# A new hand-set order for one attention and mixture-of-experts kernel, with one small product moved to a bank of its own

## The chip, the cores and the metric

The kernel runs on one core of a Trainium2 chip. The metric is the device time of one execution in microseconds (us), median of three runs.

## The reference

Attention with a sliding window of 96 keys and 8 global keys, biased by distance, over 4 batches of 8 heads with 768 positions of 64 elements; then a soft mixture of 8 experts with 4 slots each on its output.

```python
scores = scale * np.matmul(q, k.transpose(0, 1, 3, 2))
keep = is_global | is_local
bias = -slopes[:, None, None] * dist[None, :, :]
scores = np.where(keep, scores + bias, -1000000000.0)
a = np.exp(scores - np.max(scores, axis=-1, keepdims=True))
a = a / (np.sum(a, axis=-1, keepdims=True) + 1e-09)
x = np.matmul(a, v)                      # to (3072, 512), heads side by side
logits = x @ phi                         # 32 slots
d = softmax of logits over the rows      # dispatch
slot_input = d.T @ x
slot_out[e] = np.maximum(slot_input[e] @ w1[e], 0.0) @ w2[e]
out = (softmax of logits over the slots) @ slot_out
```

The window's sizes come as an integer input n (`n_global`, `n_local`), read on the device.

## The kernel before

**Two stages.** The first is attention, in 16 units u of two heads each (i = 0, 1); four units make a batch. The second, the tail, has the experts' two layers and the combination; its code is the same in both kernels and is no part of ORDER.

**Steps of one unit.** Each step is a small function that issues a few instructions:

- `load_qk`, `load_v`: one DMA each on SP's queue, into two buffers in turn (units 2 and 3 borrow weight buffers).
- `scores(u, k)`, k = 0 to 2: TensorE, 4, 4 and 6 products (two rows each in the trace, as they are float32) into one of two PSUM tiles `sc` (L535).
- `biased(u, k)`: VectorE adds a bias table to `sc`, keeps the running maximum, and writes `tb` in SBUF (L544, custom operation). One operand is in PSUM, one in SBUF.
- `max_t` (TensorE, L551) and `max_r` (VectorE, L556) turn the maximum into a bias, `exponential(u, i)` and `w_hi(u, i)` (ScalarE, L560 and L563) make exp and its float16 rounding `ph`.
- `w_lo(u, i, part)`, three parts: the rest, exp minus its rounding, 128x432 elements, two operands that both lie in SBUF (L570). `w_lo` is GpSimd's, `w_lo_dve` the same instruction on VectorE.
- `v_hi` (GpSimd, L503) or `v_hi_act` (ScalarE, L506): float16 rounding of the values; `v_lo` (VectorE, L513): the rest, again two operands in SBUF, 128x896.
- `values(u, i)`: TensorE, 39 products into bank i of the PSUM tile `x` (L587). `x` is one tile of two banks, used by all units.
- `ev_sums`, `ev_recs`: row sums and reciprocals (L600, L606). `ev_mul(u, i)`: VectorE scales bank i of `x` into `xn` and frees it (L612). These are the two scalings of a unit.
- `tr`, `tr_copy` (ScalarE, L629) or `tr_copy_dve` (VectorE, L633): transposition of `xn`; `logits` (L654).
- Each fourth unit: `logits_all` (L671), `strip_max` (L688), `strip_exp`, `strip_sum` (L705), `by_token`, `dispatch`, `dispatch_sum`: the running softmax over rows.

**At the start** `bcast` converts n and spreads it over 128 partitions with a 1-row product; `keys` reads that product and makes the limits (L816 to L818, L257 to L259), `table_even` and `table_odd` make the first bias table (L264, L268) that `biased(0, 0)` reads. `warm` issues products of ones of 512 columns, which nobody reads, into `x`; `WARM` such products stand ahead of everything (L439). In the kernel before, `bcast` writes to bank 1 of `x`, and `keys` reads it there.

**Weights.** `piece` loads a weight piece of 1 MB into a buffer of its own, `extra` loads a part of one into a corner that attention never uses (0.12 to 0.26 MB), `free` loads one into an attention buffer that is needed no more. All go by SP's one queue, in the order in which they are issued.

**What sets the order.** `ORDER` is a list of 608 steps, written out by a planner and fixed in the file. Every engine has its instructions in the order of this list, and waits by semaphores for what the others write or read. A reader or writer of a tile waits for the last step ahead of it in the list that used that tile in a conflicting way; `x` counts as one tile in this, so an `ev_mul(u, 1)` that stands behind `values(u + 1, 0)` in the list waits for that product, though it reads the other bank.

Of the kernel before, what the change touches and what calls it, by code (L numbers as in the profile page):

```python
# [49 lines left out]
WARM = 12  # L50
# [233 lines left out]
def tile_attention_moe(ctx: ExitStack, tc: tile.TileContext, qk, v, phi, w1, w2, nn, out):  # L284
    nc = tc.nc
# [70 lines left out]
    held = []  # L356
    for name, i, *_ in ORDER:
        if name == "free":
# [71 lines left out]
    ones = keep.tile([P, P], F32, name="ones")  # L430
# [6 lines left out]
    busy_in = nc.const_aps.tensor(1.0, [P, 512], BF16)  # L437
    for _ in range(WARM):
        nc.tensor.matmul(out=wp[0:1], lhsT=busy_in[:, 0:1], rhs=busy_in, start=True, stop=True)  # L439

    table = BiasTable(nc, tabs, xn01)
    nf = keep.tile([1, 4], F32, name="nf")
# [10 lines left out]
    def late_constants():  # L453
        nc.gpsimd.tensor_tensor(out=i4, in0=ident[:, 0:32], in1=ident[:, 32:64], op=ALU.add)
        nc.gpsimd.tensor_tensor(out=i4, in0=i4, in1=ident[:, 64:96], op=ALU.add)
        nc.gpsimd.tensor_tensor(out=i4, in0=i4, in1=ident[:, 96:128], op=ALU.add)
        nc.gpsimd.memset(sl, 0.0)
# [15 lines left out]
    xx = psx.tile([P, 2, 512], F32, name="x", tag="x")  # L473
    mxs, nbs, rcs, ms = {}, {}, {}, {}
# [6 lines left out]
    def bank(key):  # L481
        if key in LAST_BANKS:
            k, i = LAST_BANKS[key]
            return sc[k][:, i]
        return psm.tile([P, 512], F32, name="m", tag="m")

    class LeftBanks:

        n = 0
# [320 lines left out]
    def bcast(u):  # L810
        nc.vector.tensor_copy(out=nf, in_=nraw)
        nc.tensor.matmul(out=xx[:, 1, 0:4], lhsT=ones[0:1], rhs=nf, start=True, stop=True)

    def keys(u):
        words = xx[:, 1, 0:4].rearrange("p (i w) -> p w i", w=2)
        nc.vector.tensor_scalar(out=nlt, in0=words[:, 0], scalar1=0.0, scalar2=None, op0=ALU.is_lt)  # L816
        nc.vector.tensor_tensor(out=nlt, in0=nlt, in1=words[:, 1], op=ALU.add)
        nc.vector.scalar_tensor_tensor(out=nv, in0=nlt, scalar=2.0 ** 32, in1=words[:, 0], op0=ALU.mult, op1=ALU.add)  # L818
        table.keys(ngl, nlo)
# [10 lines left out]
    def table_pair(p):  # L830
        table.pair(p)

    steps = dict(piece=piece_of, free=free, extra=extra, load_qk0=load_qk0, load_phis=load_phis, bcast=bcast, keys=keys, table_rest=table_rest, warm_x=warm_x, warm=warm,
                 table_even=table_even, table_odd=table_odd, table_pair=table_pair, load_qk=load_qk, load_v=load_v, v_hi=v_hi, v_hi_act=v_hi_act, v_hi_dve=v_hi_dve, v_lo=v_lo,
                 scores=scores, biased=biased, max_t=max_t, max_r=max_r, exponential=exponential, w_hi=w_hi, w_lo=w_lo, w_lo_dve=w_lo_dve, w_hi_dve=w_hi_dve,
                 values=values, ev_sum=ev_sum, ev_rec=ev_rec, ev_sums=ev_sums, ev_recs=ev_recs, ev_mul=ev_mul, tr=tr, tr_copy=tr_copy, tr_copy_dve=tr_copy_dve,
                 logits=logits, logits2=logits2, logits_half=logits_half, logits_all=logits_all, strip_max=strip_max, strip_exp=strip_exp,
                 strip_sum=strip_sum, by_token=by_token, by_token_copy=by_token_copy, lnat_copy=lnat_copy, dispatch=dispatch, dispatch_sum=dispatch_sum)
    late_constants()
    for name, u, *args in ORDER:  # L840
        steps[name](u, *args)
# [291 lines left out]
```

## Time and profile before

| | |
|---|---|
| median of three runs | 209.16 us (208.80 to 209.75) |
| the profiled execution, its own time | 210.29 us |
| its span, first to last instruction | 208.4 us |
| mean granted TensorE clock | 0.958 |
| busy: TensorE, VectorE, ScalarE, GpSimd | 84%, 74%, 59%, 52% |
| attention, about | 0 to 146.6 us |
| tail, about | 146.6 to 208.4 us |

The shares are means over the whole span; attention and tail differ, and the rows below are cut by stretch. A row's "idle before" names what ended an engine's wait. Waits of an engine for a shared resource do not show as idle time in these rows: the instruction is counted as busy from its start, and becomes longer.

### The profile page before, as it was taken

How to read it: one execution, taken by the hardware profiler on the slowest of the kernel's cores; microseconds unless marked ns; L12 is line 12 of the kernel's file. 1: busy time of each engine (PE TensorE's matmuls, PEld its weight loads, DVE VectorE, ACT ScalarE, POOL GpSimd, SP SyncE). 2: the span in 40 equal slices, each digit the busy share in tenths (PEclk: the TensorE clock that was granted, in tenths of full speed). 3: DMA queues.
4: the chain of work that ended last, by engine and by line, in shares of the span. 5: the costliest groups of instructions: out<-in, count | busy, mean ns of one | idle time of the engine just before them, and what ended most of it. 6: DMA issues, size and time to landing. Idle time of an engine off the chain costs nothing.

```text
span 208.4 us, 6316 instructions
## 1 busy us (share of the span) xinstructions
PE 176.1 (84%) x2612; PEld 127.7 (61%) x2612; DVE 154.9 (74%) x382; ACT 122.1 (59%) x157; POOL 107.9 (52%) x127
## 2 busy tenths in 40 slices
PE   8879998988898999899597998698799999998400
PEld 2346777867687788788466886566443345865400
DVE  4386999998999898989798989994577804653700
ACT  3007788995958879989594889861404521531500
POOL 6302978997994988899684988790000000000000
PEclk9975999999999999999999999999999999999955
DMA  6984087499996699975948998899969999677892
GB/s 204 401 309 170 12 272 297 156 333 421 374 350 250 228 349 397 349 242 175 338 163 273 406 371 287 293 333 346 351 281 306 407 414 425 267 255 255 293 335 95
DMA packets 18761, 61.39 MB, mean 295 GB/s; under 512 B 1570, under 2 KB 8994, under 8 KB 16546
## 3 DMA queue, kind: packets, MB, share of 16 engines
q1 hardware_dynamic: 18720, 60.89, 80.1%
q8 instruction: 22, 0.36, 0.7%
q14 instruction: 17, 0.14, 0.2%
q10 hardware_dynamic: 2, 0.00, 0.0%
HBM read 54.59 MB, written 6.29 MB: 292 GB/s over the span
## 4 chain that ended last, share of the span: by engine, by line
PE 54%; DVE 28%; issue 5%; POOL 4%; DMA 3%; ACT 1%; DVEq 0%; POOLq 0%
PE x L587 11%; PE sc L535 11%; PE x L139 7%; DVE tb L544 7%; PE hp L106 7%; DVE v L513 5%; DVE xn L612 4%; POOL ph L570 3%; DMA raw<-in_qk_dram 3%; DVE ph L570 3%; PE m L624 3%; PE wp L439 3%; PE cp L199 2%; PE ctp L173 2%; PE x L524 2%
## 5 line engine op out<-in xcount | busy, mean ns | idle before, releaser
L570 POOL TENSOR_TENSOR ph<-tb,ph 128x432 f16<-128x432 f32 x82 | 92.6, 1160 | 29.3 <-ACT ph L563 28.9
L560 ACT ACTIVATE tb<-tb,nb 128x1296 f32<-128x1296 f32 x32 | 43.6, 1374 | 17.1 <-DVE nb L556 17.0
L587 PE MATMUL x<-v,ph 128*128 128x65 f16 (+1 forms) x1248 | 43.2, 193 | 6.7 <-DVE xmax L612 5.8
L587 PEld LDWEIGHTS <-ph 128*128 128x128 f16 x1248 | 41.0, 97 | 11.3 <-issue 6.0
L563 ACT CAST ph<-tb 128x1296 f16<-128x1296 f32 x32 | 40.5, 1270 | 12.6 <-PE x L587 11.3
L535 PE MATMUL sc<-raw 64*128 64x216 f32 (+1 forms) x392 | 42.7, 354 | 3.9 <-DVE mx L544 2.9
L535 PEld LDWEIGHTS sc<-raw 64*128 64x128 f32 x392 | 33.5, 195 | 11.5 <-DVE mx L544 4.9
L612 DVE CUSTOM_DVE_ANT_1 xn<-x,rc 120x448 f32<-120x448 f32 x32 | 19.4, 622 | 3.8 <-PE x L587 3.3
L513 DVE SCALAR_TENSOR_TENSOR v<-vt,v 128x896 f16<-128x896 f32 x14 | 19.3, 1377 | 0.8 <-POOL v L503 0.8
L544 DVE CUSTOM_DVE_ANT_1 tb<-sc,tt,mx 128x864 f32<-128x864 f32 x16 | 17.8, 1110 | 2.0 <-PE sc L535 1.1
L624 PE MATMUL m<-ident,xn 120*128 120x120 f32 x105 | 15.7, 275 | 1.9 <-DVE xmax L612 1.4
L570 DVE TENSOR_TENSOR ph<-tb,ph 128x432 f16<-128x432 f32 x14 | 14.4, 1032 | 0.0
L624 PEld LDWEIGHTS m<-ident,xn 120*128 120x128 f32 x105 | 10.8, 141 | 4.8 <-issue 2.1
L139 PE MATMUL x<-wp,wp 128*32 128x256 f32 x96 | 10.7, 380 | 0.0
L106 PE MATMUL hp<-wp,sl 128*32 128x512 f32 x80 | 10.5, 593 | 0.0
L503 POOL TENSOR_SCALAR v<-vt 128x896 f16<-128x896 f32 x9 | 9.6, 1065 | 1.0 <-PE x L587 1.0
L544 DVE CUSTOM_DVE_ANT_1 tb<-sc,xtt,mx 128x864 f32<-128x864 f32 x8 | 8.9, 1111 | 0.3
L544 DVE CUSTOM_DVE_ANT_1 tb<-sc,xta,mx 128x864 f32<-128x864 f32 x8 | 8.9, 1110 | 0.1
L544 DVE CUSTOM_DVE_ANT_1 tb<-sc,tt 128x864 f32<-128x864 f32 x8 | 8.4, 1052 | 0.0
L139 PE MATMUL x<-ph,wp 128*32 128x256 f32 x32 | 7.3, 380 | 0.0
L139 PE MATMUL x<-tb,wp 128*32 128x256 f32 x32 | 7.2, 379 | 0.0
L199 PE MATMUL cp<-sots,ct 128*128 128x256 f32 x48 | 6.6, 291 | 0.6 <-DVE sots L185 0.6
(207 smaller groups left out, 280.6 us busy)
## 6 DMA issues: line engine op xcount, KB each, us to landing
wp<-in_w_dram SPq DMA_DIRECT2D x11, 1024.0 KB, 9.0
raw<-in_qk_dram SPq DMA_DIRECT2D x13, 832.0 KB, 6.9
vt<-in_v_dram SPq DMA_DIRECT2D x14, 448.0 KB, 5.8
wp<-in_w_dram SPq DMA_DIRECT2D x10, 512.0 KB, 6.6
tb<-in_w_dram SPq DMA_DIRECT2D x4, 1024.0 KB, 7.5
raw<-in_w_dram SPq DMA_DIRECT2D x2, 1024.0 KB, 13.9
out_dram<-tb SPq DMA_DIRECT2D x4, 512.0 KB, 3.5
out_dram<-xtt SPq DMA_DIRECT2D x4, 512.0 KB, 7.0
```

The costliest lines, as they stand in the source:

```text
L106: nc.tensor.matmul(out=hp[n][32 * s:32 * s + 32, :], lhsT=slv(a, c, s), rhs=w1(e, c // 2)[:, (c % 2) * DF + 512 * n:(c % 2) * DF + 512 * n ...
L139: nc.tensor.matmul(out=o[32 * s:32 * s + 32, 0:w], lhsT=ht[:, c, 32 * s:32 * s + 32], rhs=w2(4 * a + s, half)[:, c0 + c * w:c0 + c * w + w ...
L199: nc.tensor.matmul(out=cp[:, w * k:w * k + w], lhsT=ct[:, t * P:t * P + P], rhs=sot, start=True, stop=True)
L513: nc.vector.scalar_tensor_tensor(out=vlo[k].rearrange("p j i d -> p (j i) d"), in0=vraws(u).rearrange("p j i d -> p (j i) d"), scalar=V_SC ...
L535: nc.tensor.matmul(out=z[:, i, at:at + n], lhsT=r_[r, KCOL[j]:KCOL[j] + KR], rhs=r_[r, KW + KB * j:KW + KB * j + n], start=True, stop=True)
L544: nc.vector.tensor_tensor_reduce(out=tb(u)[:, :, BW * k:BW * k + BW], in0=sc[(3 * u + k) % 2][:, :, 0:BW], in1=table.unit(u % NP, k), scal ...
L560: nc.scalar.activation(out=t, in_=t, func=AF.Exp, bias=nbs[u], scale=T_SC)
L563: nc.scalar.copy(out=blocks(phi_[i])[:, :, 0:QW], in_=tb(u)[:, i].rearrange("p (s c) -> p s c", c=QW))
L570: (engine or nc.gpsimd).tensor_tensor(out=blocks(plo_[i])[:, c, 0:QW], in0=tb(u)[:, i].rearrange("p (s c) -> p s c", c=QW)[:, c], in1=bloc ...
L587: nc.tensor.matmul(out=x[:, (D + 1) * t:(D + 1) * t + d], lhsT=w[:, c:c + P], rhs=vv[:, j, i, 0:d], start=(z == 0), stop=(z == len(ops) - ...
L612: nc.vector.tensor_tensor_reduce(out=xnb[(u // 2) % 3][:, :, c:c + D], in0=xv[:, i, :, 0:D], in1=rcs.pop((u, i)).unsqueeze(2).to_broadcast ...
L624: nc.tensor.transpose(out=m[:, at:at + KB], in_=xnb[(u // 2) % 3][:, t, P * (p % 2):P * (p % 2) + P], identity=ident[0:KB, 0:KB])
```

## The change

`ORDER` holds the same steps in another order, and some go to another engine. Counted in the two lists:

| step | before | after |
|---|---|---|
| `w_lo` on GpSimd / `w_lo_dve` on VectorE | 82 / 14 | 78 / 18 |
| `v_hi` on GpSimd / `v_hi_act` on ScalarE | 10 / 6 | 8 / 8 |
| `tr_copy` on ScalarE / `tr_copy_dve` on VectorE | 29 / 3 | 27 / 5 |
| products of `warm` in ORDER / of WARM | 14 / 12 | 17 / 6 |
| units whose `ev_mul` stands behind the next unit's first `values` | 7 | 0 |
| `extra` steps ahead of the first load of q and k | 0 | 2 |

```diff
-WARM = 12
-ORDER = [('load_qk0', 0), ('bcast', 0), ('warm', 0, 2), ('scores', 0, 0), ('load_qk', 0), ('warm', 0, 1),
...
+WARM = 6
+ORDER = [('bcast', 0), ('keys', 0), ('extra', 4), ('extra', 5), ('load_qk0', 0), ('warm', 0, 2), ('scores', 0, 0),
...
     def bcast(u):
         nc.vector.tensor_copy(out=nf, in_=nraw)
-        nc.tensor.matmul(out=xx[:, 1, 0:4], lhsT=ones[0:1], rhs=nf, start=True, stop=True)
+        ms["n"] = m = bank(("n", u))
+        nc.tensor.matmul(out=m[:, 0:4], lhsT=ones[0:1], rhs=nf, start=True, stop=True)
 
     def keys(u):
-        words = xx[:, 1, 0:4].rearrange("p (i w) -> p w i", w=2)
+        words = ms.pop("n")[:, 0:4].rearrange("p (i w) -> p w i", w=2)
```

`bank` gives one of the two PSUM banks `m` that transpositions and logits use.

**VectorE at the start, `bcast` and `keys`**, as a difference (x is the tile of the values and of the warm products, m a bank of its own):

```order
 L811 CAST nf<-nraw 1x4 [waits DMAHW0_49]
-L816 TENSOR_SCALAR nlt<-x 128x2 [waits PE_49]
-L817 TENSOR_TENSOR nlt<-nlt,x 128x2 [waits DVE_49]
-L818 SCALAR_TENSOR_TENSOR nv<-nlt,x 128x2 [waits DVE_49]
+L817 TENSOR_SCALAR nlt<-m 128x2 [waits PE_49]
+L818 TENSOR_TENSOR nlt<-nlt,m 128x2 [waits DVE_49]
+L819 SCALAR_TENSOR_TENSOR nv<-nlt,m 128x2 [waits DVE_49]
```

The rows are the same but for the tile: the first waits now for the product that wrote m alone, and no more for warm products that write x.

**SP's queue at the start**, before (raw, wp of in_qk are q and k, vt are values):

```order
L400 DMA raw_93<-in_qk_dram 128x592
L404 DMA raw_93<-in_qk_dram 128x432
L404 DMA raw_93<-in_qk_dram 128x640
L404 DMA raw_94<-in_qk_dram 128x1664
L404 DMA wp_91<-in_qk_dram 128x1664
L407 DMA vt<-in_v_dram 128x896
L404 DMA wp_92<-in_qk_dram 128x1664
L407 DMA vt<-in_v_dram 128x896 [waits DMAHW0_49]
```

and now:

```order
L387 DMA raw_93<-in_w_dram 128x384
L387 DMA raw_94<-in_w_dram 128x384
L400 DMA raw_93<-in_qk_dram 128x592
L387 DMA vt<-in_w_dram 128x256
L404 DMA raw_93<-in_qk_dram 128x432
L404 DMA raw_93<-in_qk_dram 128x640
L387 DMA xn_105<-in_w_dram 128x256
L404 DMA raw_94<-in_qk_dram 128x1664 [waits DMAHW0_49]
L407 DMA vt<-in_v_dram 128x896 [waits DMAHW1_49]
L387 DMA ph_98<-in_w_dram 128x512 [waits DMAHW2_49]
L404 DMA wp_92<-in_qk_dram 128x1664 [waits DMAHW3_49]
L387 DMA wp_83<-in_w_dram 128x2048 [waits DMAHW4_49]
```

Parts of weights (in_w) moved in front of and between the loads of q and k.

**VectorE around the scalings of unit 6**, before (L612 into xn is a scaling, L513 is `v_lo`):

```order
L600 TENSOR_TENSOR rsall<-x,eps 120x14 [waits PE_49]
L606 RECIPROCAL rc<-rsall 120x14 [waits DVE_49]
L556 ISA m,nb<-m,shift 128x128 [waits PE_49]
L556 ISA nb 128x1
L612 ISA xn_106,xmax<-x,rc 120x7x64 [waits DVE_49]
L612 ISA xmax 120x1
L513 SCALAR_TENSOR_TENSOR v_100<-vt,v_100 128x896 [waits DMAHW4_49]
L544 ISA tb_97,mx<-sc_177,xtt,mx 128x2x432 [waits PE_49]
L544 ISA mx 128x1
L612 ISA xn_106,xmax<-x,rc 120x7x64 [waits PE_49]
L612 ISA xmax 120x1
```

and now:

```order
L544 ISA tb_95,mx<-sc_171,tt,mx 128x2x432 [waits DVE_49,PE_49]
L544 ISA mx 128x1
L750 COPY sacc<-m 128x512 [waits PE_49]
L612 ISA xn_106,xmax<-x,rc 120x7x64
L612 ISA xmax 120x1
L612 ISA xn_106,xmax<-x,rc 120x7x64
L612 ISA xmax 120x1
L544 ISA tb_96,mx<-sc_170,xta 128x2x432 [waits PE_49,Activation_49,Pool_49]
L544 ISA mx 128x1
L513 SCALAR_TENSOR_TENSOR v_100<-vt,v_100 128x896 [waits DMAHW1_49,Activation_49]
```

The second scaling moved up to the first and lost its wait for TensorE.

## Rows read from the trace of the kernel before

**Rows 1.** Stretches: length, busy PE PEld DVE ACT POOL (count), clock, DMA share, GB/s.

```profile
0.00:13.00 13.00, 10.12 (x48) 4.48 (x49) 6.50 (x25) 1.76 (x3) 5.13 (x35) 1.00 0.87 325
13.00:19.00 6.00, 6.00 (x24) 2.93 (x26) 4.65 (x11) 2.24 (x2) 0.00 (x0) 0.54 0.64 235
...
22.00:140.00 118.00, 104.47 (x1879) 87.25 (x1878) 110.30 (x260) 96.35 (x112) 100.00 (x90) 1.00 0.81 292
...
146.60:208.40 61.80, 46.71 (x540) 26.60 (x536) 28.63 (x76) 17.00 (x34) 0.00 (x0) 0.91 0.83 307
```

**Rows 2.** Groups by line and shape, columns: count | busy us, mean ns | idle before.

```profile
L570 POOL TENSOR_TENSOR ph<-tb,ph 128x432 f16<-128x432 f32 x82 | 92.6, 1160 | 29.3 <-ACT ph L563 28.9 <-DVE mx L544 0.3
L503 POOL TENSOR_SCALAR v<-vt 128x896 f16<-128x896 f32 x9 | 9.6, 1065 | 1.0 <-PE x L587 1.0
...
L513 DVE SCALAR_TENSOR_TENSOR v<-vt,v 128x896 f16<-128x896 f32 x14 | 19.3, 1377 | 0.8 <-POOL v L503 0.8
L570 DVE TENSOR_TENSOR ph<-tb,ph 128x432 f16<-128x432 f32 x14 | 14.4, 1032 | 0.0
L513 DVE SCALAR_TENSOR_TENSOR v<-wp,v 128x896 f16<-128x896 f32 x2 | 2.9, 1426 | 0.0
```

**Rows 3.** Single lines, columns: count, duration in ns as minimum/median/maximum, first and last start.

```profile
L513 DVE SCALAR_TENSOR_TENSOR v<-vt,v x14: 1086/1192/1921, 23.1 to 134.6; 128x896 f16<-128x896 f32 x14
L570 DVE TENSOR_TENSOR ph<-tb,ph x14: 603/1098/1456, 39.3 to 139.4; 128x432 f16<-128x432 f32 x14
L570 POOL TENSOR_TENSOR ph<-tb,ph x82: 997/1009/1940, 19.5 to 139.3; 128x432 f16<-128x432 f32 x82
L705 DVE SCALAR_TENSOR_TENSOR state<-state,al x3: 214/908/967, 105.9 to 149.4; 128x1 f32<-128x1 f32 x3
L544 DVE CUSTOM_DVE_ANT_1 tb<-sc,xtt,mx x8: 1104/1110/1119, 29.7 to 128.0; 128x864 f32<-128x864 f32 x8
L633 DVE COPY xtt<-m x1: 651/651/651, 86.9 to 86.9; 128x480 f32<-128x480 f32 x1
```

**Rows 4.** Instructions in order of time, 134 to 140 us, columns: start, us, engine.

```profile
134.57 5.72 POOL L570 TENSOR_TENSOR ph<-tb,ph 128x432 f16<-128x432 f32 x5 [1.37 <-ACT ph L563]
134.61 1.92 DVE L513 SCALAR_TENSOR_TENSOR v<-vt,v 128x896 f16<-128x896 f32 x1
```

**Rows 5.** Waits: who waited for whom, columns: total us, times, longest us.

```profile
DVE xn L612 <- PE x L587: 3.3, 4, 1.4
PE x L587 <- DVE xmax L612: 5.8, 9, 1.9
```

**Rows 6.** Instructions in order of time, 99 to 102 us, the false wait.

```profile
99.87 1.33 PE L587 MATMUL x<-v,ph 128*128 128x65 f16 x39 [0.22 <-DVE xmax L612]
101.24 0.62 DVE L612 CUSTOM_DVE_ANT_1 xn<-x,rc 120x448 f32<-120x448 f32 x1 [1.43 <-PE x L587]
```

**Rows 7.** Instructions in order of time, 0 to 17 us.

```profile
0.77 5.28 PE L439 MATMUL wp<-const-bfloat16-1.0 128*1 128x512 bf16 x12 [0.77 <-PEq L1120]
3.10 0.34 DVE L811 CAST nf<-nraw 1x4 f32<-1x4 int32 x1
5.98 0.58 PE L812 MATMUL x<-nf,ones 1*128 1x4 f32 x2
7.05 1.00 PE L535 MATMUL sc<-raw 64*128 64x216 f32 x8
8.40 0.16 DVE L816 TENSOR_SCALAR nlt<-x 128x2 f32<-128x2 f32 x1 [4.96 <-PE x L524]
10.80 1.06 DVE L544 CUSTOM_DVE_ANT_1 tb<-sc,tt 128x864 f32<-128x864 f32 x1
13.45 1.81 PE L535 MATMUL sc<-raw 64*128 64x216 f32 x8
```

**Rows 8.** Issue of the first DMA of q and k: count, KB, us to landing.

```profile
raw<-in_qk_dram SPq DMA_DIRECT2D x1, 296.0 KB, 2.9
```

**Rows 9.** The chain that ended last, 36 to 48 us, columns: start, us, what.

```profile
38.14 6.54 DMA raw<-in_qk_dram
```

2 lines of the change are left out of this document (1 added, 1 removed).

## The prediction

> **What bounds the kernel now.** I read the stretches first, then the groups by line, then single durations, the waits, and the start in order of time. The stretches [rows 1] show two regimes. From 146.6 us on the tail takes 61.8 us; its code is not touched, so it counts as fixed and the change must pay in attention. From 22 to 140 us VectorE is busy 110.3 of 118 us, TensorE 104.5, GpSimd 100.0, ScalarE 96.4: VectorE is the fullest engine, and nobody has much room. From 13 to 19 us the granted clock is 0.54, so that eight score rows that took 1.00 us at 7.05 take 1.81 us at 13.45 [rows 1, 7].
>
> VectorE's busy time is not all work. `v_lo` takes 1.09 us at best and 1.92 us at worst, `w_lo` 0.60 and 1.46 us on VectorE, 1.00 and 1.94 us on GpSimd [rows 3]. `biased` stays within 1.10 to 1.12 us [rows 3], though GpSimd works beside it most of the time. What tells them apart is that `v_lo` and `w_lo` have two operands in SBUF, `biased` one. The order of time shows how: a `v_lo` that starts 0.04 us behind a GpSimd subtraction takes 1.92 us, about one GpSimd instruction (1.01) plus its own 1.09 less the overlap of start and end [rows 3, 4]. So the two engines take turns, instruction by instruction, and whoever comes second waits inside its own busy time. Summed, with the shortest duration as the work: `v_lo` 22.2 us busy - 16 x 1.09 = 4.8 us of waiting; VectorE's `w_lo` 14.4 - 14 x 0.603 = 6.0; two of the three state sums (L705) 0.91 and 0.97 for 0.21 = 1.4. VectorE waits 12.2 us in 32 instructions, 0.38 each; GpSimd's `w_lo` wait 92.6 - 82 x 1.009 = 9.9 us [rows 2, 3].
>
> Put end to end, this exclusive work is 82 x 1.009 + 10 x 1.065 on GpSimd and 17.4 + 8.4 on VectorE, 119 us, in the about 121 us from 19.5 to 140.3 [rows 2, 3]. Starts and ends overlap a little, so the turn-taking is not full, but it is the fullest resource of all.
>
> **Start.** The 12 products of WARM start 0.44 us apart (5.28 / 12) and `bcast`'s product follows at 5.98 [rows 7]. Six fewer free it 2.6 us sooner; the converted n is there at 3.44 [rows 7], so the product can start near 3.5 and end at 4.1. Then `keys` waits for nothing else: the 4.96 us wait on warm products in x goes [rows 7]. From `keys` to the first `biased` took 10.80 - 8.40 = 2.4 us, so the table is there at 6.5. The other input is `scores(0, 0)`. Its 296 KB landed 2.9 us after their issue [rows 8]; now two parts of weights of 192 KB (384 columns of float32) go first: two issues of about 0.45 us and 0.39 MB, which at 325 GB/s [rows 1] is 1.2 us if it all adds. I take landing at 5.0 (4.5 to 5.7), the scores 1.0 to 1.8 us later, and the first `biased` at 6.8 in place of 10.80: 4 us ahead. Not all of it reaches the steady part, since the next scores wait for more of q and k behind two more weight parts, and since the clock may be half from the beginning: three score blocks at 1.81 for 1.00 are 2.4 us. If the clock instead never falls from 13 to 19 us, up to 5 blocks x 0.8 = 4 us come on top, less what the load order takes. Ends -0.7 and -6; I take **-3.5 us**, near the undisturbed 4.
>
> **Work moved.** Four `w_lo` more on VectorE: +4 x 0.603 = 2.4 us there, -4 x 1.009 = 4.0 on GpSimd. Two `tr_copy_dve` more: at most +2 x 0.65 = 1.3 us [rows 3]. Two `v_hi` move from GpSimd (-2 x 1.065 = 2.1) to ScalarE, which has 21 us free [rows 1, 2]. VectorE gets +3.7 us of work, and the exclusive work falls by 4.0 + 2.1 - 2.4 = 3.7 us.
>
> **Scalings ahead of the next product.** In seven units the second `ev_mul` stood behind the next unit's first product and waited for it. At 101.24 VectorE waits 1.43 us for a product that started at 99.87 [rows 6]; four such waits sum to 3.3 us [rows 5]. They go. The price: in those seven units the next `values` now starts after the second scaling as well, 0.54 us later where TensorE was waiting already; it does wait there, 5.8 us in 9 times [rows 5]. That is 0 to 7 x 0.54 = 3.8 us on TensorE, which has 13.5 us of room in the stretch; I take **+1.0 us** on the end.
>
> **Two-operand work apart.** The trace of before can't show how well the new order separates it. One bound: nothing gained, 36 instructions at 0.38 (the two state sums aside) = 13.7 us of waiting, +1.5 more than now. The other: all 12.2 us gone. I take half, 6 us: the order of both engines is fixed and they hang together through ScalarE and TensorE, but a turn is 1 us long, and half a turn of drift undoes a placement. So VectorE's time in the stretch changes by +3.7 - 3.3 - 6 = -5.6 us. It does not all reach the end, because the chain there alternates between TensorE and VectorE; half is 2.8. The exclusive work, the other candidate for the bound, falls by 3.7. Both point to **-3.0 us** (ends +1.9 and -8).
>
> [...]
>
> **End of attention and tail.** Of unit 15's six `w_lo` GpSimd does three in place of five, VectorE three in place of one: 5 x 1.009 + 0.603 = 5.6 us in turn becomes 4.8. As the last products wait for them I take **-0.5 us**. Weights come earlier in SP's queue (`extra` and `piece` steps moved forward), and the tail's own loads are unchanged: 0.
>
> **Sum.** -3.5 + 1.0 - 3.0 - 0.5 = -6.0 us against the profiled execution's 210.29, so 204.3. That execution is 1.13 us above the median of the three runs, 209.16; on that scale the forecast is **203.2 us**, for its own case 201.5 to 205.
>
> **Rivals.** *The separation is perfect*: all 12.2 us go, VectorE's stretch falls by 3.7 - 3.3 - 12.2 = -11.8, half reaches the end, -5.9 in place of -3.0: 200.3. For it: the durations fall into two clear levels [rows 3], so a planner can know them. Against: drift. *The clock stays half from the start*, since the warm-up is halved: the lead is 4 - 2.4 = 1.6 us in place of 3.5: 205.1. For it: the clock was low after a pause of TensorE already [rows 1, 7]; against: ORDER has three more warm products among the first scores. [...] *The loads become the wait*: weight pieces go between the loads of q and k, and one such load already holds the chain for 6.54 us [rows 9]. If half the start's lead (1.8) and half the steady gain (1.5) are spent waiting for q and k, 206.5. Against: DMA is busy 0.81 of the steady stretch [rows 1], and all ten pieces come early, so the later loads have a freer queue. *Slower: the order comes apart at run time.* Turns are granted as before, 0.38 us a piece: VectorE +3.7 - 3.3 + 1.5 = +1.9, all of it passed on as the engine is full; the seven later products cost their 3.8; the lead shrinks to 1.6; the end gives 0.5: +3.6, so 212.8. It decides once drift exceeds about half a turn, 0.5 us, at most placements. That the change does nothing is no case: the start's wait is gone for certain.
>
> **How the numbers follow.** Forecast 0.42, perfect separation 0.15, low clock 0.15, loads 0.18, order comes apart 0.10. About 0.5% (1.05 us) is what a measurement can tell from no change. Faster by more holds the first three wholly and most of the fourth: 0.82; within 0.5%, its rest and a mild form of the last, 0.09; slower 0.09. The range, 199.2 to 208.2, takes in the first four with their unknown terms and leaves out the best of the second and the slower case.
>
> **What would show it.** First `biased` near 6.8 us, not 10.8; granted clock from 13 to 19 us above 0.54; `v_lo` on average below 1.25 us and VectorE's `w_lo` below 0.85 (now 1.38 and 1.03); no wait of L612 for L587; VectorE's busy time up to the end of attention a few us lower, and attention's end near 140.5; the tail unchanged at 61.8 us. The forecast is wrong if `v_lo` and `w_lo` keep their means, if TensorE's waits for q and k or for the scalings grow past 5 us, or if the tail starts to wait for weights.

## The result and the profile after

The changed kernel takes 202.84 us (median of four runs, 201.58 to 204.56), the kernel before 209.45 us beside it (208.80 to 210.02): a ratio of 0.969, 95% interval 0.961 to 0.977. The forecast was 203.2 us. Ratios, here and below, leave out runs over 1.5% longer than the fastest of the same kernel, which matters for one version alone (e9, four of its six runs). The profiled execution of after took 204.56 us, with a span of 202.6 in place of 208.4; the readings below compare these two spans, which differ by 5.8 us.

The stretches of after, to be held against [rows 1] (length, busy PE PEld DVE ACT POOL with counts, clock, DMA share, GB/s):

```profile
0.00:13.00 13.00, 9.05 (x44) 4.48 (x44) 7.62 (x27) 1.95 (x4) 5.33 (x35) 0.90 0.83 278
13.00:19.00 6.00, 6.00 (x45) 3.63 (x43) 4.88 (x12) 4.00 (x4) 0.52 (x1) 0.93 1.01 417
...
140.60:202.60 62.00, 46.97 (x542) 26.69 (x540) 28.54 (x76) 16.80 (x33) 0.00 (x0) 0.91 0.85 316
```

The clock from 13 to 19 us is 0.93 where it was 0.54, the DMA share there 1.01 where it was 0.64. From 10 to 13 us it went the other way, 0.58 in place of 1.00, and the third block of scores took 1.95 us in place of 1.08. Attention ends at 140.6 in place of 146.6, and the tail takes 62.0 us, as before (61.8). The start of after, in order of time (start, us, engine), answers [rows 7]:

```profile
3.58 0.38 PE L813 MATMUL m<-nf,ones 1*128 1x4 f32 x2
4.01 0.16 DVE L817 TENSOR_SCALAR nlt<-m 128x2 f32<-128x2 f32 x1 [0.57 <-PE m L813]
...
6.77 1.06 DVE L544 CUSTOM_DVE_ANT_1 tb<-sc,tt 128x864 f32<-128x864 f32 x1
...
9.32 1.00 PE L535 MATMUL sc<-raw 64*128 64x216 f32 x8 [1.96 <-DMA raw<-in_qk_dram]
...
10.36 1.12 DVE L544 CUSTOM_DVE_ANT_1 tb<-sc,tt,mx 128x864 f32<-128x864 f32 x1 [2.08 <-PE sc L535]
...
10.56 1.95 PE L535 MATMUL sc<-raw 64*128 64x216 f32 x12
```

The first `biased` starts at 6.77 us, 4.0 us ahead. Then the second block of scores waits 1.96 us for its part of q and k, VectorE waits 2.08 us for that block, and the fourth `biased` starts at 15.55, only 1.0 us ahead of the 16.55 of before.

From that fourth `biased` to the end of attention, before and after (columns as above):

```profile
16.55:146.60 130.05, 115.70 (x2017) 94.77 (x2015) 117.59 (x277) 103.31 (x121) 102.81 (x92) 0.99 0.79 287
```

```profile
15.55:140.60 125.05, 113.70 (x2018) 94.20 (x2015) 119.01 (x283) 103.66 (x120) 95.66 (x86) 1.00 0.80 297
```

So of the 5.8 us the start kept 1.0, the stretch gave 5.0, and the tail took 0.2 back. In the stretch VectorE is busy no less than before (119.01 against 117.59). What fell is its time without work: 130.05 - 117.59 = 12.5 us, now 125.05 - 119.01 = 6.0. GpSimd is busy 7.2 us less.

The groups of two-operand work (count | busy us, mean ns | idle before) and their single lines (minimum/median/maximum in ns), to be held against [rows 2, 3]:

```profile
L570 POOL TENSOR_TENSOR ph<-tb,ph 128x432 f16<-128x432 f32 x78 | 86.8, 1145 | 30.4 <-ACT ph L563 30.0
...
L513 DVE SCALAR_TENSOR_TENSOR v<-vt,v 128x896 f16<-128x896 f32 x14 | 19.4, 1383 | 0.0
...
L570 DVE TENSOR_TENSOR ph<-tb,ph 128x432 f16<-128x432 f32 x18 | 16.2, 916 | 0.0
```

```profile
L513 DVE SCALAR_TENSOR_TENSOR v<-vt,v x14: 1078/1090/1894, 20.8 to 131.1; 128x896 f16<-128x896 f32 x14
L513 DVE SCALAR_TENSOR_TENSOR v<-wp,v x2: 1565/1668/1772, 31.3 to 37.1; 128x896 f16<-128x896 f32 x2
```

Counted as the prediction did, with 1.09 us and 0.603 us as the work: `v_lo` waits 14 x 1.383 + 2 x 1.668 - 17.4 = 5.3 us inside itself, VectorE's `w_lo` 18 x 0.916 - 18 x 0.603 = 5.6. That is 10.9 us in 34 steps, where it was 4.8 + 6.0 = 10.8 us in 30: 0.32 us a step after 0.36. The waiting in turns is what it was. Waits of TensorE (total us, times, longest us), beside [rows 5]; no row of L612 waiting for L587 is left:

```profile
PE sc L535 <- DMA raw<-in_qk_dram: 3.9, 3, 2.0
...
PE x L587 <- DVE xmax L612: 2.2, 5, 0.6
```

### The profile page after: what moved, and what is told of

Same layout as the page of the kernel before. It is cut to its first block, busy times and chain, and to the rows that moved or that the text cites. A ratio compares the mean times of both kernels' runs of the same rounds, so it can differ in the third digit from the quotient of the medians.

```text
span 202.6 us, 6321 instructions
## 1 busy us (share of the span) xinstructions
PE 172.3 (85%) x2609; PEld 126.9 (63%) x2609; DVE 156.6 (77%) x388; ACT 123.2 (61%) x157; POOL 101.0 (50%) x121
## 4 chain that ended last, share of the span: by engine, by line
## 5 line engine op out<-in xcount | busy, mean ns | idle before, releaser
L570 POOL TENSOR_TENSOR ph<-tb,ph 128x432 f16<-128x432 f32 x78 | 86.8, 1145 | 30.4 <-ACT ph L563 30.0
L587 PE MATMUL x<-v,ph 128*128 128x65 f16 (+1 forms) x1248 | 43.4, 193 | 5.9 <-POOL ph L570 2.4
L587 PEld LDWEIGHTS <-ph 128*128 128x128 f16 x1248 | 41.2, 97 | 8.8 <-issue 3.8
L535 PE MATMUL sc<-raw 64*128 64x216 f32 (+1 forms) x392 | 41.1, 346 | 4.0 <-DMA raw<-in_qk_dram 3.9
L535 PEld LDWEIGHTS sc<-raw 64*128 64x128 f32 x392 | 33.0, 192 | 11.6 <-issue 5.7
L513 DVE SCALAR_TENSOR_TENSOR v<-vt,v 128x896 f16<-128x896 f32 x14 | 19.4, 1383 | 0.0
L612 DVE CUSTOM_DVE_ANT_1 xn<-x,rc 120x448 f32<-120x448 f32 x32 | 18.9, 620 | 0.5
L570 DVE TENSOR_TENSOR ph<-tb,ph 128x432 f16<-128x432 f32 x18 | 16.2, 916 | 0.0
L506 ACT ACTIVATE v<-vt 128x896 f16<-128x896 f32 x7 | 6.6, 948 | 11.1 <-DMA vt<-in_v_dram 11.1
L503 POOL TENSOR_SCALAR v<-vt 128x896 f16<-128x896 f32 x7 | 7.8, 1114 | 0.5 <-PE x L587 0.5
```

The lines of the kernel that those rows point to most:

```text
L503: nc.gpsimd.tensor_scalar(out=vhi[u % 2][:, :, :, 0:D], in0=vraws(u), scalar1=V_SC, scalar2=0.0, op0=ALU.mult, op1=ALU.add)
L513: nc.vector.scalar_tensor_tensor(out=vlo[k].rearrange("p j i d -> p (j i) d"), in0=vraws(u).rearrange("p j i d -> p (j i) d"), scalar=V_SC ...
L535: nc.tensor.matmul(out=z[:, i, at:at + n], lhsT=r_[r, KCOL[j]:KCOL[j] + KR], rhs=r_[r, KW + KB * j:KW + KB * j + n], start=True, stop=True)
L570: (engine or nc.gpsimd).tensor_tensor(out=blocks(plo_[i])[:, c, 0:QW], in0=tb(u)[:, i].rearrange("p (s c) -> p s c", c=QW)[:, c], in1=bloc ...
L587: nc.tensor.matmul(out=x[:, (D + 1) * t:(D + 1) * t + d], lhsT=w[:, c:c + P], rhs=vv[:, j, i, 0:d], start=(z == 0), stop=(z == len(ops) - ...
L612: nc.vector.tensor_tensor_reduce(out=xnb[(u // 2) % 3][:, :, c:c + D], in0=xv[:, i, :, 0:D], in1=rcs.pop((u, i)).unsqueeze(2).to_broadcast ...
```

## The experiments

### The start

**The start alone, on the kernel before (e2).** All loads stay where they were.

```diff
-WARM = 12
-ORDER = [('load_qk0', 0), ('bcast', 0), ('warm', 0, 2), ('scores', 0, 0), ('load_qk', 0), ...
+WARM = 6
+ORDER = [('bcast', 0), ('keys', 0), ('load_qk0', 0), ('warm', 0, 2), ('scores', 0, 0), ('load_qk', 0), ...
-        nc.tensor.matmul(out=xx[:, 1, 0:4], lhsT=ones[0:1], rhs=nf, start=True, stop=True)
+        ms["n"] = m = bank(("n", u))
+        nc.tensor.matmul(out=m[:, 0:4], lhsT=ones[0:1], rhs=nf, start=True, stop=True)
```

> The kernel before with the start alone: n's product in its own bank, its two steps first in the list, 6 warm products in place of 12; all loads where they were. Theory that the loads of weights ahead of q and k ate the changed kernel's lead (4.0 us at the first bias step, 1.0 at the fourth): here nothing is put ahead of q and k, so the first bias step starts at 5.5 to 6.8 us, the fourth 2 to 4 us ahead of 16.55, and the time falls by 2 to 4 us, 205.5 to 207.5. Rival (the lead is lost to a lower clock after the short warm-up, or absorbed later): the fourth bias step is at most 1 us ahead, and the time is 208.4 or above.

205.14 us against 209.48, ratio 0.979 (0.975 to 0.983): 4.3 us. In order of time:

```profile
6.88 1.06 DVE L544 CUSTOM_DVE_ANT_1 tb<-sc,tt 128x864 f32<-128x864 f32 x1 [0.24 <-PE sc L535]
7.28 1.81 PE L535 MATMUL sc<-raw 64*128 64x216 f32 x8
...
9.14 1.12 DVE L544 CUSTOM_DVE_ANT_1 tb<-sc,tt,mx 128x864 f32<-128x864 f32 x1 [0.76 <-PE sc L535]
...
13.11 1.05 DVE L544 CUSTOM_DVE_ANT_1 tb<-sc,tt 128x864 f32<-128x864 f32 x1
```

The first `biased` is no earlier than in the changed kernel, and two blocks of scores even run at half speed (1.81 us). But no block waits for a load: the fourth `biased` starts at 13.11, 3.4 us ahead of the kernel before. The theory of the loads holds so far.

**The changed kernel with its first weight parts behind the first loads (e5).**

```diff
-ORDER = [('bcast', 0), ('keys', 0), ('extra', 4), ('extra', 5), ('load_qk0', 0), ('warm', 0, 2), ('scores', 0, 0), ('extra', 6), ('load_qk', 0), ('table_even', 0), ('extra', 0), ...
-... ('load_v', 0), ('extra', 1), ...
+ORDER = [('bcast', 0), ('keys', 0), ('load_qk0', 0), ('warm', 0, 2), ('scores', 0, 0), ('load_qk', 0), ('table_even', 0), ...
+... ('load_v', 0), ('extra', 4), ('extra', 5), ('extra', 6), ('extra', 0), ('extra', 1), ...
```

> The changed kernel with its four early weight parts (extra 4, 5, 6, 0) set behind the first loads of q, k and v of units 0 and 1 (behind load_v 0); nothing else moved. The start alone on the kernel before, with no weights ahead of q and k, kept 4.7 to 5.2 us of lead to the end of attention. If the weight parts cost the changed kernel 1.5 to 2.5 us of its start: second block of scores without a wait for its load (1.96 us there), fourth bias step at 13 to 14 us in place of 15.55, time 200.3 to 201.3 us. Rival (a later wait, for values or for weights in the tail, takes the lead back): 202.3 us or more.

200.54 us against 209.31, ratio 0.961 (0.956 to 0.966). In order of time, and the stretch from the fourth `biased` to the end of attention:

```profile
6.69 1.00 PE L535 MATMUL sc<-raw 64*128 64x216 f32 x8
6.78 1.06 DVE L544 CUSTOM_DVE_ANT_1 tb<-sc,tt 128x864 f32<-128x864 f32 x1
...
8.19 1.11 DVE L544 CUSTOM_DVE_ANT_1 tb<-sc,tt,mx 128x864 f32<-128x864 f32 x1
...
11.40 1.05 DVE L544 CUSTOM_DVE_ANT_1 tb<-sc,tt 128x864 f32<-128x864 f32 x1
```

```profile
11.40:136.50 125.10, 113.83 (x2019) 94.19 (x2015) 118.18 (x283) 103.69 (x120) 95.22 (x86) 1.00 0.83 311
```

The second block follows at once (6.69 in place of 9.32), and the fourth `biased` is 4.15 us earlier than in the changed kernel. From there to the end of attention both take the same 125.1 us: the lead of the start passes through untouched, and no weight comes late to the tail (136.5 to the end of the span at 198.4 is 61.9 us). In medians the gain is 2.3 us.

Part of the 4.15 us is chance. In the execution of after the third block of scores ran at half speed (the row at 10.56), in that of e5 none of the first six did. The same start with weights ahead, in the execution of e4 (whose edit comes later in the list), has the first block at half speed:

```profile
6.41 1.81 PE L535 MATMUL sc<-raw 64*128 64x216 f32 x8 [1.33 <-DMA raw<-in_qk_dram]
...
14.28 1.05 DVE L544 CUSTOM_DVE_ANT_1 tb<-sc,tt 128x864 f32<-128x864 f32 x1
```

So the start is better read from all kept traces. Its fourth `biased` comes at 15.84 to 16.64 us with the start of before (before, e1, e6; mean 16.34), at 13.12 to 15.55 with that of after (after, e4, e7, e8, e10, e11; mean 14.09), at 11.39 to 13.43 with no weights ahead of q and k (e2, e3, e5, e9, e12; mean 12.15). By these means the new start is worth 4.19 us, the weights ahead cost 1.94 of it, and the changed kernel keeps 2.25, not 1.0.

Of the versions that compute the reference only the next one is as fast as this.

**Loads later still (e12).** As the last, with these parts and the first 1 MB piece behind `load_v` of unit 1.

```diff
-... ('load_v', 0), ('extra', 4), ('extra', 5), ('extra', 6), ('extra', 0), ('extra', 1), ('v_hi_act', 0), ('load_qk', 2), ... ('piece', 0), ('load_v', 1), ...
+... ('load_v', 0), ('v_hi_act', 0), ('load_qk', 2), ... ('load_v', 1), ('extra', 4), ('extra', 5), ('extra', 6), ('extra', 0), ('extra', 1), ('piece', 0), ...
```

> As e5, with the early weight parts (extra 4, 5, 6, 0, 1 and the first 1 MB piece) set behind the loads of q, k of units 0 to 2 and v of units 0 and 1. In e5 the first score block of unit 2 still waits 1.52 us for its load, at 21.25 us. If that wait is on the path: it goes, and the time is 199 to 200 us. If VectorE's own work holds that stretch anyway, or a later wait for weights takes it back: 200.3 us or more.

Ratio 0.960 (0.955 to 0.965), median 201.74: not to be told from the last. The edit missed its wait. The block that waits 1.52 us in e5 is the tenth, at three a unit, so it belongs to unit 3 and not to unit 2, and the load of unit 3 still stands behind the weights. First that block in e5, then the same in e12, then the load of unit 3 in e12 (KB, us to landing):

```profile
21.25 1.00 PE L535 MATMUL sc<-wp 64*128 64x216 f32 x8 [1.52 <-DMA wp<-in_qk_dram]
```

```profile
22.14 1.81 PE L535 MATMUL sc<-wp 64*128 64x216 f32 x8 [2.49 <-DVE mx L544]
```

```profile
wp<-in_qk_dram SPq DMA_DIRECT2D x1, 832.0 KB, 9.9
```

In e12 this load is issued at 12.08 us (10.65 in e5) and lands at about 22.0, and the block starts later, not earlier. The row of e12 names VectorE as what ended the wait; but in e5 the same block started at 21.25, while that bias step still ran (20.99 to 22.09), so it was the load here too. What the wait is worth stays open.

### The scalings

**The late scaling ahead of the next product (e1).** On the kernel before, in seven units, as here in unit 2:

```diff
-('values', 3, 0), ('ev_mul', 2, 1)
+('ev_mul', 2, 1), ('values', 3, 0)
```

> The kernel before with one part of the change alone: in its seven units the late scaling stands ahead of the next unit's first values product. Book-keeping theory (VectorE had 11.06 us without work between its fourth bias step and the end of attention, 3.84 of it in front of L612; the changed kernel has 6.45 and 0.52, at the same busy time): this part alone is worth 3.3 us, so about 206.1 us against 209.45, ratio 0.984, and VectorE's idle time in front of L612 below 1 us. Rival (the whole new list is needed): TensorE pays the 0.54 us per unit back, its waits for L612 rise from 5.8 us to 8 or more, and the time stays within 1 us, 208.5 or above.

216.48 us against 209.48, ratio 1.035 (1.032 to 1.039): 7 us slower, which neither theory expected. On VectorE hardly a row moved; only the wait turned round, and the scaling stands where it stood, up to four instructions behind the first one. Units 3 and 4, in order of time:

```profile
53.49 0.62 DVE L612 CUSTOM_DVE_ANT_1 xn<-x,rc 120x448 f32<-120x448 f32 x1
...
54.33 1.22 DVE L570 TENSOR_TENSOR ph<-tb,ph 128x432 f16<-128x432 f32 x1 [0.20 <-ACT ph L563]
...
57.48 0.61 DVE L612 CUSTOM_DVE_ANT_1 xn<-x,rc 120x448 f32<-120x448 f32 x1
...
58.16 1.88 PE L587 MATMUL x<-v,ph 128*128 128x65 f16 x39 [2.10 <-DVE xmax L612]
```

```profile
58.00:60.10 2.10, 1.94 (x41) 1.85 (x41) 0.10 (x2) 0.00 (x0) 0.28 (x1) 0.67 0.96 332
```

```profile
PE x L587 <- DVE xmax L612: 14.4, 11, 2.1
```

The product waits for a scaling 4 us behind the first one, and then takes 1.88 us at a granted clock of 0.67 (the stretch from 58 to 60.1 us), where such products take about 1.35 at 1.00. TensorE's waits for scalings rise from 5.8 us to 14.4. The kernel before had its false wait for a reason: it let the product go first.

**The same with the start (e3).** The edits of e1 and e2 together.

> Both parts together on the kernel before, without any other replanning. If the parts add and the replanned separation brings nothing: 202.5 to 204.5 us, as fast as the changed kernel (202.84). If the new list's other moves bring the prediction's 3 us: 205.5 to 207, at least 2.5 us slower than the changed kernel.

211.31 us, ratio 1.010 (1.006 to 1.015). The start gives about as much as it does alone (216.48 - 211.31 = 5.2); the loss of the other part stays.

**The second scaling right behind the first (e6).** The form that the changed kernel has in 13 of its 16 units, again on the kernel before in its seven units:

```diff
-('ev_mul', 2, 0), ('exponential', 4, 1)
+('ev_mul', 2, 0), ('ev_mul', 2, 1), ('exponential', 4, 1)
-('values', 3, 0), ('ev_mul', 2, 1)
+('values', 3, 0)
```

> The kernel before with the second scaling of the seven units right behind the first, as in the changed kernel. (In the earlier run e1 it stood only ahead of the product, so up to four other VectorE instructions ran between the two scalings while TensorE waited.) If distance between the scalings was what cost e1 its 7 us: TensorE waits at most 7 x 0.54 = 3.8 us more, VectorE's 3.3 us of waiting go, and the time is 206 to 208.5 us. Rival (any delay of the first product hurts this list, since exp, rounding and GpSimd hang on it, and TensorE's clock falls when it waits): 210.5 us or more.

207.67 us against 209.31, ratio 0.990 (0.986 to 0.994): 1.6 us by the medians, 2.1 by the ratio. The price on TensorE does not come:

```profile
PE x L587 <- DVE xmax L612: 5.9, 7, 1.9
```

5.9 us after 5.8, and no row of L612 waiting for L587 is left. So it was the distance between the scalings that cost 7 us, and placed side by side they are worth half of the wait that they remove.

**The scalings behind the product, in the changed kernel (e4).** In units 6, 7, 8, 10, 11, 12 and 13, as here in unit 6:

```diff
-('ev_mul', 6, 1), ('scores', 10, 0)
+('scores', 10, 0)
-('values', 7, 0)
+('values', 7, 0), ('ev_mul', 6, 1)
```

> The changed kernel with the second scaling of seven units (6, 7, 8, 10, 11, 12, 13) set behind the next unit's first values product again. Book-keeping theory: VectorE waits for L587 again, 0.5 to 0.8 us a unit, 3 to 5 us in all, and the time rises by about 3.3 to 206 us. Rival (in the new list other work covers it, and TensorE gains the 0.54 us per unit): below 204 us.

208.74 us, ratio 0.997 (0.993 to 1.000), 5.9 us above the changed kernel. The stretch from the fourth `biased` to the end of attention, and VectorE's wait:

```profile
14.28:145.00 130.72, 114.78 (x2019) 94.42 (x2015) 120.54 (x283) 104.28 (x120) 95.56 (x86) 1.00 0.78 291
```

```profile
DVE xn L612 <- PE x L587: 4.2, 5, 1.4
```

The wait is back with 4.2 us, and the stretch is 130.7 us long, no shorter than in the kernel before. The edit also moves the scaling past other VectorE work, so the whole 5.9 us is not the wait alone.

**Start and adjacent scalings, on the kernel before (e9).** The edits of e2 and e6 together.

> The kernel before with the start of e2 (n's product in its own bank, first in the list, 6 warm products) and the adjacent scalings of e6, nothing else replanned. The two alone gave 4.3 and 1.6 us. If they add: 203 to 204 us, and the changed kernel with its loads put first (e5, 200.54) owes about 3 us to the rest of the new list. If the rest of the new list is worth nothing: 200 to 201.5 us. If the two spoil each other: 205 us or more.

Six runs spread from 201.43 to 207.17 us, median 205.33, and the ratio is 0.965 (0.958 to 0.973). The product of the two parts alone is 0.979 x 0.990 = 0.970. So these two edits bring the kernel before about to where the changed kernel stands (0.969). What the rest of the new list is worth can't be read from this run: against the version with its loads first (0.961) the ratios leave 0.9 us for it, and with both intervals anything from -1.0 to 2.8.

**The scalings and the rest of the list, from the traces.** From the tenth `biased` on the start plays no part any more, and the clock is 0.99 or 1.00. From there to the end of attention, first the kernel before, then with adjacent scalings (e6), the new list with the scalings behind the product (e4), and the changed kernel:

```profile
27.18:146.60 119.42, 105.33 (x1915) 87.72 (x1915) 108.35 (x260) 94.45 (x114) 96.02 (x86) 1.00 0.84 304
```

```profile
25.99:144.50 118.51, 107.19 (x1915) 89.47 (x1915) 106.77 (x260) 94.61 (x114) 94.86 (x87) 0.99 0.84 308
```

```profile
24.90:145.00 120.10, 105.09 (x1892) 87.60 (x1892) 109.92 (x265) 94.66 (x113) 87.87 (x80) 1.00 0.76 280
```

```profile
26.17:140.60 114.43, 104.00 (x1891) 87.36 (x1892) 108.39 (x265) 94.04 (x113) 87.97 (x80) 1.00 0.78 286
```

The new list with its scalings set back is no shorter than the old one (120.1 after 119.4 us), the scalings alone give 0.9 us here, and both together 5.0. So the two parts do not simply add: the rest of the list pays with the scalings adjacent. These are single executions, and e4 moves more than the wait, so the share of each stays open.

### The turns

**No two-operand work on GpSimd (e7).** Each `w_lo` of GpSimd becomes two copies with one operand.

```diff
-        (engine or nc.gpsimd).tensor_tensor(out=blocks(plo_[i])[:, c, 0:QW], in0=tb(u)[:, i]...,
-                                            in1=blocks(phi_[i])[:, c, 0:QW], op=ALU.subtract)
+        for _ in range(2):
+            nc.gpsimd.tensor_scalar(out=blocks(plo_[i])[:, c, 0:QW], in0=blocks(phi_[i])[:, c, 0:QW], scalar1=1.0, scalar2=0.0, op0=ALU.mult, op1=ALU.add)
```

> The changed kernel without two-operand work on GpSimd: each of its 78 subtractions w_lo is left out and replaced by two instructions with one SBUF operand over the same 128x432 elements (a copy of the rounded weights, done twice, so that GpSimd is busy about as long, 1.0 to 1.1 us). It prices all the turn-taking that the separation could have saved. Expected by every theory: v_lo at 1.09 us and VectorE's w_lo at 0.60 us each time, 10 to 13 us less busy time on VectorE. If turn-taking is on the path that sets the end, half or more of it comes back: 196.5 us or less. If it is hidden beside other waits: 200.5 us or more.

206.09 us, ratio 0.984 (0.980 to 0.989), slower than the changed kernel, and what the expectation took as common to every theory failed. Groups, single lines, and TensorE's wait for GpSimd's part (total us, times, longest us):

```profile
L572 POOL TENSOR_SCALAR ph<-ph 128x432 f16<-128x432 f16 x156 | 98.0, 643 | 23.8 <-ACT ph L563 17.3
...
L574 DVE TENSOR_TENSOR ph<-tb,ph 128x432 f16<-128x432 f32 x18 | 13.4, 755 | 0.0
```

```profile
L513 DVE SCALAR_TENSOR_TENSOR v<-vt,v x14: 1084/1095/1803, 19.4 to 133.1; 128x896 f16<-128x896 f32 x14
L572 POOL TENSOR_SCALAR ph<-ph x156: 545/551/1485, 17.1 to 135.6; 128x432 f16<-128x432 f16 x156
```

```profile
PE x L591 <- POOL ph L572: 6.9, 11, 1.2
```

VectorE's two-operand steps still wait, for GpSimd instructions with one operand as well, and these wait in turn (0.55 us, up to 1.49). The waiting on VectorE halves, 10.9 to 14 x 1.252 + 2 x 1.271 - 17.4 + 18 x (0.755 - 0.603) = 5.4 us, and the instruction waited for is about half as long (0.55 us after 1.01). But GpSimd's part takes 98.0 us in place of 86.8, and TensorE waits 6.9 us for it where it waited 2.4. That fits a GpSimd whose own time holds the products back, which no run tested by itself; the turns weren't priced.

**VectorE's steps with one operand (e10).** Changed kernel, `v_lo` and `w_lo_dve` without their subtraction.

```diff
-        nc.vector.scalar_tensor_tensor(out=vlo[k]..., in0=vraws(u)..., scalar=V_SC, in1=vhi[k]..., op0=ALU.mult, op1=ALU.subtract)
+        nc.vector.tensor_scalar(out=vlo[k]..., in0=vraws(u)..., scalar1=V_SC, scalar2=None, op0=ALU.mult)
+        if engine is not None:
+            engine.tensor_scalar(out=blocks(plo_[i])[:, c, 0:QW], in0=tb(u)[:, i]..., scalar1=1.0, scalar2=None, op0=ALU.mult)
+            return
```

> The changed kernel with the 34 two-operand steps of VectorE (16 v_lo, 18 w_lo) cut to one operand: the subtraction of the rounded value is left out, the elements stay the same. GpSimd keeps its work. This prices the turn-taking from VectorE's side without making GpSimd's work longer, which spoiled e7. Expected by all: v_lo at 0.9 to 1.1 us and VectorE's w_lo at 0.45 to 0.6 us each time, GpSimd's w_lo at 1.01 each time, 12 to 16 us less VectorE time. If turn-taking is on the path that sets the end: 197 us or less. If it is hidden beside other waits: 200.5 us or more.

195.12 us, ratio 0.930 (0.924 to 0.935), 7.7 us below the changed kernel. Single lines and groups, then the stretch from the fourth `biased` to the end of attention:

```profile
L513 DVE TENSOR_SCALAR v<-vt x14: 616/624/1431, 18.4 to 121.9; 128x896 f16<-128x896 f32 x14
L570 DVE TENSOR_SCALAR ph<-tb x18: 321/859/1195, 31.8 to 124.9; 128x432 f16<-128x432 f32 x18
```

```profile
L570 DVE TENSOR_SCALAR ph<-tb 128x432 f16<-128x432 f32 x18 | 14.6, 826 | 0.0
L513 DVE TENSOR_SCALAR v<-vt 128x896 f16<-128x896 f32 x14 | 12.3, 876 | 0.0
```

```profile
13.12:131.60 118.48, 113.32 (x2021) 93.86 (x2018) 110.01 (x283) 103.13 (x121) 87.49 (x86) 1.00 0.86 323
```

The one-operand forms are shorter than expected (0.62 and 0.32 us at best) and wait all the same, up to 1.43 and 1.20 us: the turns are still there. Counted as above, with 0.616 and 0.321 us as the work and 1.180 us as the mean of the other two `v_lo`, VectorE waits 4.8 + 9.1 = 13.9 us inside these steps, 0.41 each. So a single operand in SBUF does not spare a step the wait, as the prediction concluded from `biased`, and this run doesn't price the turns alone either. It says something else: with VectorE 119.01 - 110.01 = 9.0 us less busy and GpSimd 8.2 us less, the stretch is 125.05 - 118.48 = 6.6 us shorter. How much of that each engine brought is not told apart.

**Shifted (e8).** The changed kernel with VectorE's two-operand steps one place on, as here `v_lo` of unit 0:

```diff
-('v_lo', 0), ('biased', 2, 1)
+('biased', 2, 1), ('v_lo', 0)
```

> The changed kernel with every two-operand step of VectorE exchanged with a neighbour on that engine: of the 34 steps (16 v_lo, 18 w_lo) 27 stand one VectorE step later, 7 one earlier. If the new list's placing of two-operand work against GpSimd's saves anything, the shift undoes it: waiting inside v_lo and w_lo rises from 12.1 us (0.36 a step) to 16 or more, time 205 us or more. If the turns come as chance has them (GpSimd is in such work for about 0.7 of the time, half an instruction of 1.0 us left on average, 0.35 us a step): waiting stays at 10 to 14 us, time 201.5 to 204.5 us.

220.71 us, ratio 1.054. In four steps (`v_lo` of units 3 and 15, a `w_lo` of 14 and of 15) the shift crossed a load, and part of what they read was overwritten and waited for, so the time is not to be used. The waiting inside `v_lo` and `w_lo` is: 14 x 1.310 + 2 x 1.586 - 17.4 + 18 x (1.004 - 0.603) = 11.3 us, after 10.9 in the changed kernel.

**Shifted again (e11),** with no step moved past a load: the same edit for nearly all of the 34 steps, 12 of them moved earlier.

> As e8, but with no step moved past a load or past another user of its buffers, which e8 did near the end: 20 of VectorE's 34 two-operand steps one VectorE step later, 12 one earlier, 2 where they were. If the new list's placing saves turns: waiting inside v_lo and w_lo rises from 12.1 us to 16 or more. If turns come as chance has them: 10 to 14 us, as in e8 (10.9), and what the time rises by stands in TensorE's waits for v_lo and w_lo instead. Time: 203 to 210 us by both.

214.96 us, ratio 1.027 (1.020 to 1.033), 12 us above the changed kernel. Groups:

```profile
L570 DVE TENSOR_TENSOR ph<-tb,ph 128x432 f16<-128x432 f32 x18 | 19.1, 1080 | 0.5 <-ACT ph L563 0.5
...
L563 ACT CAST ph<-tb 128x1296 f16<-128x1296 f32 x32 | 40.4, 1271 | 21.1 <-PE x L587 15.9 <-PE m L551 1.9 <-POOL ph L570 1.3
```

The waiting inside `v_lo` and `w_lo` is 14 x 1.319 + 2 x 1.614 - 17.4 + 18 x (1.080 - 0.603) = 12.9 us, 0.38 a step: within what chance gives (10 to 14), and 2 us above the changed kernel's. The rest goes with longer waits around the products: ScalarE's rounding, which needs the buffers that `values` frees, waits 15.9 us for TensorE (8.6 in the changed kernel), and TensorE itself 5.4 us for scalings (2.2) and 3.4 us for VectorE's `w_lo` (0.2). These waits overlap, so they are no sum. Placing decides a lot here, and only about 2 of the 12 us stand in the turns.

## Why the prediction was right, and where it was not

**Time:** right, 203.2 forecast and 202.84 measured. That the number is so close is luck. In the profiled executions the start brought 1.0 us for 3.5 forecast, the rest of attention 5.0 for 2.5 (1.0 - 3.0 - 0.5), and the two errors cancel; and the reason given for the term of -3.0 fell.

**Start, -3.5 us:** the first `biased` came at 6.77 for 6.8 forecast, and the clock from 13 to 19 us rose to 0.93. But the changed kernel kept only 1.0 us of it at the fourth `biased` in the profiled execution, 2.25 us by the means over all traces. The main cause is the one that the third rival named, q and k behind weights: moving the weight parts back gave 2.3 us by the medians (1.94 by the means of the traces). The start without them is worth 4.3 us on the kernel before. Of the second rival, a low clock at the start, the slow blocks are there too, not every time: one or two of the first three blocks ran at half speed (1.6 us and more where others take 1.0 to 1.1) in 7 of the 11 traces of the new start, and none in those of e3, e5, e10 and e12. The clock of the profile shows it in part: 0.58 from 10 to 13 us in the changed kernel, where the third block takes 1.95 us, but 1.00 from 0 to 13 us in e2, where the first two take 1.81 us each. No run varied the warm-up alone, so that its halving slows these blocks was not shown. The term was right for the edit and too large for the edit together with the loads put ahead of it.

**Work moved:** `w_lo` and `v_hi` left GpSimd as counted; its busy time in the stretch fell by 7.2 us for 6.1 forecast.

**Scalings:** the wait of L612 for L587 is gone. The price of +1.0 us on TensorE did not come: its waits for scalings are 5.9 us after 5.8 with adjacent scalings on the kernel before, and 2.2 in the changed kernel. Alone the edit gives 1.6 to 2.1 us. The prediction's net for it, half of 3.3 less 1.0, was 0.65. It did not see that the same edit with the scalings apart costs 7 us.

**Two-operand work apart:** this step failed. Half of the waiting was to go; 10.8 us became 10.9, and only the 1.4 us of the state sums went. `v_lo` is at 1.42 us on average, above the 1.25 given as the mark, VectorE's `w_lo` at 0.92, above 0.85. The first end of the bound, turns as before, held: 0.32 us a step after 0.36, and 0.38 with nearly every step shifted. That two operands in SBUF are what tells the waiting steps from `biased` did not hold either: with one operand they wait 0.41 us each (e10). VectorE's busy time did not fall by a few us, as the prediction wanted, but rose by 1.4. A slip in this part of the working changes no result: its 36 instructions include the two state sums that it says it sets aside (34 at 0.38 are 12.9 us).

**What stood in for it:** VectorE's idle time in the stretch fell by 12.5 - 6.0 = 6.4 us, of which the scalings' false wait is 3.3. On the kernel before, the scalings alone shortened the time by about 2 us; with them adjacent, the rest of the new list brings about 4 us more (118.5 to 114.4 us from the tenth `biased` on, though the ratio of e9 allows less), and without them nothing (e4). What it is in the rest of the list is argued, not shown: it takes 7.2 us from GpSimd's busy time, and its steps are placed so that products wait less, as the shifted run suggests by losing 12 us. The two were not told apart. So attention behind the start gained more than the terms of +1.0, -3.0 and -0.5 together, for a reason that was not the one given.

**Tail, 0, and end of attention:** 62.0 us for 61.8, attention's end 140.6 for 140.5. The 0.5 us of unit 15 was not measured by itself.

**The marks:** "wrong if `v_lo` and `w_lo` keep their means" was the wrong mark for the time. `v_lo` kept its mean and `w_lo` fell only from 1.03 to 0.92, and the time came. The other marks did not go off: TensorE waited 3.9 us for q and k and 2.2 us for the scalings, and the tail took 62.0 us after 61.8.

## What to carry to other kernels

Where two engines take turns, an order fixed in advance did not lower the waiting: it stayed at 0.32 to 0.38 us a step in the four lists counted here, so plan with such a price, taken from your own trace, and cut the work that takes turns. A wait that looks false can be what lets the next engine start early: here it paid to remove it only where the work that it held back moved up beside what it belongs to: the same dependency was worth -1.6 us with the scalings adjacent and +7.0 us with them apart. And loads for later belong behind the first loads of the main loop: a lead won at the start ran through to the end of attention here (125.05 and 125.10 us from the fourth `biased` on), and putting four weight parts behind those loads was worth 2.3 us by the medians. A start whose blocks run at half speed in one execution and not in the next moved single profiles by 2 us (the fourth `biased` at 13.12 to 15.55 with the same start), so read it from several.

## What the runs showed of the hardware

VectorE's turns with GpSimd are not a matter of two operands on both sides: beside one-operand GpSimd instructions of 0.55 us each a two-operand VectorE step waits (e7: `w_lo` at 0.755 on average for 0.603), and a one-operand VectorE step from SBUF to SBUF that runs at 0.32 us at best beside GpSimd's two-operand `w_lo` takes up to 1.20 us (e10). `biased`, with one operand in PSUM, stays at 1.02 to 1.12 us beside GpSimd's `w_lo` in the changed kernel.

TensorE's speed at the start differs between executions of the same instructions: the first block of scores takes 1.00 us in the profile of the changed kernel and 1.81 us in those of e4, e7, e8 and e11, which issue the same up to there. The profile's clock does not show it in e4: it reads 1.00 from 0 to 13 us.
